# Output weights and two raw blocks loaded between the first two groups' values, with the first decode steps tied to the first group's chain

## The chip, the core and the metric

The kernel runs on one core of a Trainium2 chip. The metric is the device time of one execution, in microseconds (us). The core has TensorE (PE, matmuls), VectorE (DVE), ScalarE (ACT), GpSimd (POOL) and SyncE (SP), which here issues nearly all DMA transfers. Each engine works through its own list of instructions in order, and an instruction that waits for a semaphore holds up everything behind it on that engine.

## What is computed

Three layers follow one another for a batch of B = 8 sequences of S = 576 tokens (cut from the reference):

```python
# 1. packed attention: 8 heads of 64, 32 packed queries p per head
p_packed = softmax(p @ k.T / 8) @ v
x = softmax(q @ p_packed.T / 8) @ p_packed           # (8, 576, 512)
# 2. four experts of causal attention, head size 64; the top 2 of 4 by gate
for e in range(4):
    a = causal_softmax((x @ wq[e]) @ (x @ wk[e]).T / 8)
    out += gate[e] * (a @ (x @ wv[e]) @ wo[e])
# 3. a channel mix with token shift
xk = mu_k * x + (1 - mu_k) * x_prev;  xr = mu_r * x + (1 - mu_r) * x_prev
result = sigmoid(xr @ w_r) * (relu(xk @ w_k) ** 2 @ w_v)
```

`w_k`, `w_v` and `w_r` arrive as 64-bit floats, so the kernel reads them as pairs of 32-bit words ("raw" blocks) and decodes them.

## The kernel before

The first half (to about 410 us) runs the attention and the experts, batch by batch. A batch has two groups of four heads. The function `front` carries one group through a chain of small steps that pass from engine to engine: scores against the packed queries (`s1`, PE), their maximum and exponential (DVE, ACT), transposes `aT` (PE, ACT), the values (`vn`, PE) to `pp` (DVE), its transpose `ppT` (PE, ACT), the second scores `s2` of the queries `qT` (PE), their 32x32 transposes to the tile `st` (DVE, L303), maximum, subtraction (L308), exponential (ACT), sums, scaling, a transpose to `a2` and a split of it into two parts `A2h` (ACT) and `A2l` (DVE, L329). `PWh` and `PWl` (L315) come from the weights `wa` in the same way. After both groups, `values` (L352) and `project` (L407) use these on PE; `project` hands the queries and keys to `soft` (L466) by copies on ACT, DVE and POOL (`qs`, in `evac`, L202) and four small DMAs (L428, L429).

Beside this, `fold` multiplies the output weights `wo` into `w_k` and `w_r`. It loads `wo` into the tile `won`, splits it on POOL into `woTh` (L202) and `woTl` (L646), and then takes the weight in blocks of 128 rows and 256 columns. For a block, `decode` (L598) reads a `raw` tile: four DVE steps `dce`, `dcx`, `dce`, `dcu` (L611 to L620), an addition on POOL (`dcx`, L626), a square on ACT (`dcq`, L630), and a last DVE step that writes the block into `wc` (L640). Then POOL splits `wc` into `wh` and `wl`, and PE multiplies (L695). The tiles `won` and `wc` share one buffer (tag `wc`, one copy), so the first write to `wc` waits until POOL has finished with `won`. After four blocks of a piece POOL splits scaled blocks once more (`wh` x4 and `wl` x4) for a second set of matmuls.

The second half multiplies by `w_r` (L854), `w_k` (L874) and `w_v` (L915).

The order in which steps are written comes from a list sorted by times in units of an expert's block: `add(kind, generator, times)`; `FOLD_T` and `FOLD_N` give the fold's times, 13 of them up to 10.15. The tile framework then schedules the instructions of each engine by priorities and an estimate of its own, so a step need not stand where its time says. The first batch's front steps have a high priority (`PR0`), its loads are all written at the first step, and the DMAs run through eight completion semaphores in turn: a ninth DMA is issued only when the first has landed.

Of the kernel before, what the change touches and what calls it, by code (L numbers as in the profile page):

```python
# [9 lines left out]
F32 = mybir.dt.float32  # L10
# [3 lines left out]
AF = mybir.ActivationFunctionType  # L14
ALU = mybir.AluOpType
# [15 lines left out]
OUT_LAG = [3.85, 4.64, 7.81]  # L31
FOLD_T = [-20.0, 10.15, 107.63]
FOLD_N = 13
WA_AT = -28.3
# [17 lines left out]
def f32(ap):  # L52
    return ap.bitcast(F32)
# [3 lines left out]
def kernel(  # L57
# [4 lines left out]
    nc = tc.nc  # L62
    P = 128
# [9 lines left out]
    NDT = DM // P  # L73
# [21 lines left out]
    def nm(s):  # L95
        uid[0] += 1
        return f"{s}_{uid[0]}"
# [43 lines left out]
    if True:  # L141
# [59 lines left out]
        def pool_copy(o, x):  # L201
            nc.gpsimd.tensor_scalar(o, x, 1.0, 0.0, op0=ALU.mult, op1=ALU.add)  # L202

        def evac(eng, o, x):
            if eng == "A":
                nc.scalar.copy(o, x)  # L206
            elif eng == "V":
                nc.vector.tensor_copy(o, x)
            else:
                pool_copy(o, x)  # L210

# [18 lines left out]
        def load(b, gs):  # L230

            for g in gs:
                pT = pTs[(b * NG + g) % 2]
                nc.sync.dma_start(pT, p[b, g].rearrange("d j n -> d (j n)"))
                kT = ld.tile([P, NH, SH], F32, tag="kT", name=nm("kT"))
                nc.sync.dma_start(kT, k[b, g])
                loaded[b, g] = [pT, kT]
            for g in gs:
                vn = vns[(b * NG + g) % 2]
                nc.sync.dma_start(  # L240
                    vn[:, : NT - 1, :], v[b, g, : (NT - 1) * P].rearrange("(c p) x -> p c x", p=P)
                )
                nc.sync.dma_start(vn[TAIL:, NT - 1, :], v[b, g, (NT - 1) * P :])
                qT = ld.tile([P, NH, SH], F32, tag="qT", name=nm("qT"))
                nc.sync.dma_start(qT, q[b, g])
                loaded[b, g] += [vn, qT]

        def front(b, g):
# [33 lines left out]
            for c in range(NT):  # L282
# [7 lines left out]
            pp = fr.tile([P, 2, D], F32, tag="pp", name=nm("pp"))  # L290
            nc.vector.tensor_scalar(
                pp, ps[:, :D].unsqueeze(1).to_broadcast([P, 2, D]), ri, None, op0=ALU.mult
            )
            yield
            ps = one()
            nc.tensor.transpose(ps[:, :P], pp.rearrange("p x d -> p (x d)"), ident)
            ppT = fr.tile([P, P], F32, tag="ppT", name=nm("ppT"))
            evac(E_PPT, ppT, ps[:, :P])
# [8 lines left out]
            small = nc.gpsimd if b else nc.vector  # L307
            small.tensor_tensor(  # L308
                st3, st3, m2.unsqueeze(2).to_broadcast([P, NCB, NPK]), op=ALU.subtract
            )  # L310
            nc.scalar.activation(st, st, AF.Exp, scale=SC)
            yield
# [13 lines left out]
            a2 = fr.tile([P, S], F32, tag="sa", name=nm("a2"), bufs=4)  # L326
            nc.vector.transpose(a2, st)
            evac("P" if b else "A", bat["A2h"][:, g, :], a2)
# [269 lines left out]
        def decode(dst, src, r0, f0, raw=None):  # L598

            if src.dtype != I64:
# [7 lines left out]
            }  # L610
            nc.vector.tensor_scalar(  # L611
                t["e"], hi, 3, 0x3FFFFFF8, op0=ALU.logical_shift_left, op1=ALU.bitwise_and
            )
            nc.vector.scalar_tensor_tensor(
# [14 lines left out]
            if E_SQ == "A":  # L629
                nc.scalar.activation(f32(t["q"]), f32(hi), AF.Square)  # L630
            else:
                nc.gpsimd.tensor_mul(f32(t["q"]), f32(hi), f32(hi))
# [22 lines left out]
        def fold():  # L655

            won = dv.tile([P, NDT, 2 * P], F32, tag="wc", name=nm("won"), bufs=1)
            nc.sync.dma_start(won, wo.rearrange("(c p) n -> p c n", p=P))  # L660
            woT = {x: dv.tile([P, NDT, 2 * P], F32R, name="woT" + x, bufs=1) for x in "hl"}
# [5 lines left out]
            for n_, src, f0, m in PIECES:  # L667
                wc, wh, wl = quad()
                for c in range(NDT):
                    decode(wc[:, c, :], src, c * P, f0)  # L670
                    split(wh[:, c, :], wl[:, c, :], wc[:, c, :])
                    yield
# [66 lines left out]

        bats, loaded = {}, {}  # L740
        steps = []
# [196 lines left out]
        swap = max(last, FOLD_T[2] + 0.1)  # L938
        add("k", call(swap_w), [swap])
# [150 lines left out]
```

## Time and profile before

| | us |
|---|---|
| median of 3 runs | 827.92 |
| lowest and highest of these | 823.35, 831.87 |
| the profiled execution: its time | 830.5 |
| the profiled execution: its span | 828.7 |

The rows further on come from that one profiled execution. Its time is 1.8 us more than its span, which the profile does not show. Each engine's busy time, the chain of waits and a timeline of instructions by start time are views of the same trace. Line numbers are those of the kernel before.

### The profile page before, as it was taken

Reading aid. Unit: us, or ns where it says so; the run is one execution under the profiler, and the core shown is the slowest. Engines: PE = TensorE matmul, PEld = TensorE weight load, DVE = VectorE, ACT = ScalarE, POOL = GpSimd, SP = SyncE. Lnnn points to the kernel's source line nnn. Section 1 sums busy time; section 2 is a strip of 40 time slices with the busy share of each in tenths; the row PEclk is TensorE's granted clock in tenths of the full one; section 3 lists DMA queues with packets and bytes.
Section 4 is the critical chain, followed back from the end, with each engine's and each line's share of the span. In section 5 each row is a group of like instructions: output and inputs, shape, how many; then the busy total and the mean of one; then the engine's idle time right before and its main releaser. Section 6 shows DMA issues by size and latency. Waiting matters only on the chain.

```text
span 828.7 us, 15307 instructions
## 1 busy us (share of the span) xinstructions
PE 774.5 (93%) x5504; PEld 623.5 (75%) x5504; DVE 485.7 (59%) x1172; ACT 479.6 (58%) x1093; POOL 380.8 (46%) x490
## 2 busy tenths in 40 slices
PE   5388999999999899989899899999999999999998
PEld 4176877859678596868677778888888888888886
DVE  1979787786868767675764777787584111111111
ACT  2258768677686777787743523242678855565400
POOL 4647757484674735233601236171166343434510
PEclk8579999999999999999999989999999999999999
DMA  9646383564745345112744958586889755555521
GB/s 323 208 137 204 115 229 113 159 182 119 202 123 168 106 126 168 49 49 78 222 146 140 335 205 292 181 275 202 310 281 309 231 170 183 190 152 185 150 66 51
DMA packets 89835, 147.81 MB, mean 178 GB/s; under 512 B 6816, under 2 KB 61600, under 8 KB 87456
## 3 DMA queue, kind: packets, MB, share of 16 engines
q1 hardware_dynamic: 89616, 146.84, 56.1%
q8 instruction: 44, 0.72, 0.4%
q14 instruction: 31, 0.25, 0.1%
q10 hardware_dynamic: 144, 0.00, 0.0%
HBM read 87.04 MB, written 50.33 MB: 166 GB/s over the span
## 4 chain that ended last, share of the span: by engine, by line
PE 68%; DVE 13%; DMA 8%; ACT 6%; issue 2%; POOL 2%; SPq 1%; DVEq 0%; POOLq 0%; ACTq 0%
PE one L915 24%; PE big L874 8%; PE one L874 8%; PE one L548 4%; PE big L407 4%; PE one L854 3%; PE one L352 3%; PE one L695 3%; DVE ms L478 3%; DMA dl<-dscr 3%; ACT ms L482 2%; PE one L466 2%; PE big L854 2%; PE one L505 2%; DMA won<-in_wo_dram 1%
## 5 line engine op out<-in xcount | busy, mean ns | idle before, releaser
L920 DVE TENSOR_TENSOR ring<-one,ring 128x512 f32<-128x512 f32 x36 | 24.9, 692 | 168.8 <-PE one L915 161.4
L915 PE MATMUL one<-wvh,yh 128*128 128x512 f32 x288 | 112.0, 389 | 0.0
L915 PE MATMUL one<-wvl,yh 128*128 128x512 f32 x288 | 112.0, 389 | 0.0
L915 PE MATMUL one<-wvh,yl 128*128 128x512 f32 x288 | 112.0, 389 | 0.0
L482 ACT ACTIVATE ms<-ms,nb 64x64 f32<-64x64 f32 (+4 forms) x160 | 89.5, 560 | 26.1 <-DVE nb L478 24.1
L206 ACT COPY tb<-one 64x128 f32<-64x128 f32 (+5 forms) x208 | 64.0, 354 | 20.3 <-PE one L512 19.4
L548 PE MATMUL one<-tb,vg 128*64 128x320 f32 (+4 forms) x448 | 64.9, 379 | 6.5 <-ACT tb L206 4.3
L626 POOL TENSOR_TENSOR dcx<-dcx,dcu 128x256 f32<-128x256 f32 x40 | 30.6, 765 | 83.7 <-DVE dcu L620 72.0
L213 POOL TENSOR_TENSOR yl<-yvh,yh 128x1024 fp32r<-128x1024 f32 (+1 forms) x24 | 49.1, 2064 | 43.3 <-ACT yh L900 25.5
L478 DVE CUSTOM_DVE_ANT_0 ms<-one,mstrip 64x64 f32<-64x64 f32 (+3 forms) x128 | 51.7, 421 | 18.6 <-PE one L466 16.4
L915 PEld LDWEIGHTS one<-wvh,yl 128*128 128x128 f32 x288 | 54.1, 188 | 11.3
L915 PEld LDWEIGHTS one<-wvl,yh 128*128 128x128 f32 x288 | 54.1, 188 | 11.3
L915 PEld LDWEIGHTS one<-wvh,yh 128*128 128x128 f32 x288 | 54.1, 188 | 11.0
L548 PEld LDWEIGHTS one<-tb,vg 128*64 128x64 f32 x448 | 37.0, 140 | 31.6 <-ACT tb L206 6.9
L505 PE MATMUL one<-ident,ms 128*128 128x128 f32 x320 | 56.0, 284 | 3.9 <-ACT tb L206 2.6
L213 POOL TENSOR_TENSOR yl<-yvl,yh 128x1024 fp32r<-128x1024 f32 x16 | 38.2, 2399 | 41.2 <-ACT yh L900 19.7
L505 PEld LDWEIGHTS one<-ident,ms 128*128 128x128 f32 x320 | 38.2, 142 | 20.8 <-ACT tb L206 7.0
L213 POOL TENSOR_TENSOR dt<-cb 128x192 f32<-128x192 f32 (+1 forms) x48 | 29.9, 652 | 34.8 <-DVE cb L565 18.4
L466 PE MATMUL one<-ks,qs 128*128 128x64 f32 (+3 forms) x128 | 41.7, 350 | 2.3 <-ACT aT L206 0.9
L630 ACT ACTIVATE dcq<-raw 128x256 f32<-128x256 f32 x40 | 17.5, 437 | 42.1 <-DMA raw<-in_w_v_dram 19.2
L466 PE MATMUL one<-kl,qs 128*128 128x64 f32 (+3 forms) x128 | 40.3, 315 | 0.0
L1037 ACT ACTIVATE ring<-ring 128x1024 f32<-128x1024 f32 x18 | 19.1, 1061 | 35.4 <-DMA ring<-rscr 35.4
(206 smaller groups left out, 2084.2 us busy)
## 6 DMA issues: line engine op xcount, KB each, us to landing
yscr<-y SPq DMA_DIRECT2D x48, 384.0 KB, 3.5
dl<-dscr SPq DMA_DIRECT2D x40, 256.0 KB, 5.4
yvh<-yscr SPq DMA_DIRECT2D x10, 1024.0 KB, 5.7
kT<-in_k_dram SPq DMA_DIRECT2D x16, 576.0 KB, 4.5
qT<-in_q_dram SPq DMA_DIRECT2D x16, 576.0 KB, 5.1
rscr<-rr SPq DMA_DIRECT2D x12, 768.0 KB, 4.6
ring<-rscr SPq DMA_DIRECT2D x36, 256.0 KB, 2.9
out_dram<-ring SPq DMA_DIRECT2D x36, 256.0 KB, 3.2
```

Source lines behind the costliest of these rows:

```text
L206: nc.scalar.copy(o, x)
L213: nc.gpsimd.tensor_tensor(o, x, y, op=op)
L407: nc.tensor.matmul(ps[:, 512 * hf : 512 * hf + SH], ww[:, g, :], xx[:, g, :], start=i == 0, stop=i == 3 * NG - 1,)
L466: nc.tensor.matmul(ps[:, po : po + kn], qs[:, i * P : i * P + P], keys[:, ko : ko + kn], start=x == 0, stop=x == 1,)
L478: nc.vector.tensor_tensor_reduce(halves(mv) if last else mv, sv, halves(mk) if last else mk, op0=ALU.add, op1=ALU.min, scale=-SC, scalar=3 ...
L482: nc.scalar.activation(mv, mv, AF.Exp, bias=nb[p0:], scale=-1.0, accum_out=bat["sums"][p0:, i, e : e + 1],)
L505: nc.tensor.transpose(ps[:, at + j * P : at + (j + 1) * P], ms[:, j * P : (j + 1) * P], ident)
L548: nc.tensor.matmul(av[64 * ee : 64 * ee + 64, qo - lo : hi - lo], vg[:, j, HD * (2 * ep + ee) : HD * (2 * ep + ee + 1)], tslice(tabs[ee], ...
L626: nc.gpsimd.tensor_add(f32(t["x"]), f32(t["x"]), f32(t["u"]))
L854: nc.tensor.matmul(po, dx[:, NS * t + s, t0 : t0 + P], wpart("r", s, wx, t), start=n == 0, stop=n == 3 * KT - 1,)
L874: nc.tensor.matmul(po.rearrange("p (b n) -> p b n", b=2), wpart("k0" if f < 4 else "k1", s, wx, t)[:, f % 4 * P : f % 4 * P + P], dx[:, :, ...
L915: nc.tensor.matmul(ps, a[:, f, P * t : P * t + P], wres["v"][b][:, f, :], start=n == 0, stop=n == 3 * NFT - 1,)
```

## The change

The DMAs of `won` and of the first two raw blocks are issued inside `load`, ahead of the second group's values and queries in the first batch. `mark` remembers five instructions of the first group's chain: on DVE the `pp` step, the subtraction in `st` and the transpose to `a2`, on ACT the copy to `ppT` and the exponential in `st`. The first DVE step and the ACT step of the first four decodes are placed behind one of them on their engine (`tc.issue_after`): on DVE block 0 behind `pp`, block 1 behind the subtraction, blocks 2 and 3 behind the transpose; on ACT blocks 0 and 1 behind `ppT`, blocks 2 and 3 behind the exponential. The first 13 fold times are listed one by one.

```diff
-FOLD_T = [-20.0, 10.15, 107.63]
-FOLD_N = 13
+FOLD_0 = [-24.0, -20.0, -19.0, -14.9, -12.5, -8.3, -6.0, -4.0, -2.5, -0.5, 1.5, 3.5, 6.5]
+FOLD_T = [10.15, 107.63]
...
             for g in gs:
+                if b == 0 and g == 1:
+                    first["won"] = dv.tile([P, NDT, 2 * P], F32, tag="wc", name=nm("won"), bufs=1)
+                    nc.sync.dma_start(first["won"], wo.rearrange("(c p) n -> p c n", p=P))
+                    first["raw"] = [fetch_raw(w_k, c * P, 0) for c in range(2)]
                 vn = vns[(b * NG + g) % 2]
...
+        def mark(b, g, eng, x, ins):
+
+            if b == 0 and g == 0:
+                for turn in {"V": [(0,), (1,), (2, 3)], "A": [(0, 1), (2, 3)]}[eng][x]:
+                    first[eng, turn] = ins.ins
...
+        def behind(ins):
+            return tc.issue_after(ins) if ins is not None else nullcontext()
+
+        def decode(dst, src, r0, f0, raw=None, turn=None):
...
-            nc.vector.tensor_scalar(
-                t["e"], hi, 3, 0x3FFFFFF8, op0=ALU.logical_shift_left, op1=ALU.bitwise_and
-            )
+            with behind(first["V", turn] if turn is not None else None):
+                nc.vector.tensor_scalar(
+                    t["e"], hi, 3, 0x3FFFFFF8, op0=ALU.logical_shift_left, op1=ALU.bitwise_and
+                )
...
-                nc.scalar.activation(f32(t["q"]), f32(hi), AF.Square)
+                with behind(first["A", turn] if turn is not None else None):
+                    nc.scalar.activation(f32(t["q"]), f32(hi), AF.Square)
...
-                    decode(wc[:, c, :], src, c * P, f0)
+                    decode(wc[:, c, :], src, c * P, f0, first["raw"].pop(0) if first["raw"] else None, c if f0 == 0 and m == 0 else None)
...
-        add("fold", fold(), even(FOLD_T[0], FOLD_T[1], FOLD_N) + even(FOLD_T[1], FOLD_T[2], NFOLD - FOLD_N))
+        add("fold", fold(), FOLD_0 + even(FOLD_T[0], FOLD_T[1], NFOLD - len(FOLD_0)))
```

On SyncE's list, from the first group's values on (`vn`, `qT`: values and queries; `wa`: the input weights), before:

```order
L240 DMA vn_125<-in_v_dram 128x4x256
L243 DMA vn_125<-in_v_dram 64x256
L245 DMA qT_166<-in_q_dram 128x1152
L240 DMA vn_126<-in_v_dram 128x4x256
L243 DMA vn_126<-in_v_dram 64x256
L245 DMA qT_170<-in_q_dram 128x1152
L196 DMA wa<-in_w_in_dram 128x1544 x2
L660 DMA won_220<-in_wo_dram 128x4x256
L761 DMA raw_313<-in_w_k_dram 128x512
L761 DMA raw_372<-in_w_k_dram 128x512
L234 DMA pT_127<-in_p_dram 128x128
```

and changed:

```order
L243 DMA vn_125<-in_v_dram 128x4x256
L246 DMA vn_125<-in_v_dram 64x256
L248 DMA qT_166<-in_q_dram 128x1152
L240 DMA won_168<-in_wo_dram 128x4x256
L774 DMA raw_170<-in_w_k_dram 128x512
L774 DMA raw_172<-in_w_k_dram 128x512
L243 DMA vn_126<-in_v_dram 128x4x256
L246 DMA vn_126<-in_v_dram 64x256
L248 DMA qT_176<-in_q_dram 128x1152
L196 DMA wa<-in_w_in_dram 128x1544 x2
L233 DMA pT_127<-in_p_dram 128x128
```

`won` and the two raw blocks moved from behind `wa` to ahead of the second group's values.

On VectorE's list, from the first group's `pp` step on (`dce`, `dcx`, `dcu`, `wc`: the decode; `st`, `m`: the first group's second scores and their maximum), before:

```order
L291 TENSOR_SCALAR pp_253<-one_232,ri_15_191 128x128
L271 RECIPROCAL ri_23_218<-su_22_215 128x1
L611 TENSOR_SCALAR dce_316<-raw_313 128x256
L614 SCALAR_TENSOR_TENSOR dcx_315<-raw_313,dce_316 128x256
L617 TENSOR_SCALAR dce_316<-dcx_315 128x256
L620 SCALAR_TENSOR_TENSOR dcu_317<-raw_313,dce_316 128x256
L611 TENSOR_SCALAR dce_375<-raw_372 128x256
L303 STREAM_TRANSPOSE st_303<-big_294 128x288 x2
L291 TENSOR_SCALAR pp_284<-one_263,ri_23_218 128x128
L306 TENSOR_REDUCE m_37_306<-st_303 128x18
L640 SCALAR_TENSOR_TENSOR wc_310<-dcq_318,dcx_315 128x256
L308 TENSOR_TENSOR st_303<-st_303,m_37_306 128x576
```

and changed:

```order
L300 TENSOR_SCALAR pp_265<-one_244,ri_18_197 128x128
L624 TENSOR_SCALAR dce_318<-raw_170 128x256
L280 RECIPROCAL ri_26_226<-su_25_223 128x1
L627 SCALAR_TENSOR_TENSOR dcx_317<-raw_170,dce_318 128x256
L630 TENSOR_SCALAR dce_318<-dcx_317 128x256
L633 SCALAR_TENSOR_TENSOR dcu_319<-raw_170,dce_318 128x256
L654 SCALAR_TENSOR_TENSOR wc_314<-dcq_320,dcx_317 128x256
L312 STREAM_TRANSPOSE st_307<-big_298 128x288 x2
L300 TENSOR_SCALAR pp_292<-one_271,ri_26_226 128x128
L315 TENSOR_REDUCE m_39_310<-st_307 128x18
L317 TENSOR_TENSOR st_307<-st_307,m_39_310 128x576
L624 TENSOR_SCALAR dce_358<-raw_172 128x256
```

Block 0's whole decode, with its last step that writes `wc`, now stands ahead of the transposes to `st`; block 1's first step, which stood ahead of them, now follows the subtraction.

On GpSimd's list, where `project` hands over the first queries (`qs`; `wh`, `wl`: the second split of the first piece), before:

```order
L626 TENSOR_TENSOR dcx_916<-dcx_916,dcu_918 128x256
L202 TENSOR_SCALAR qs_112<-qs_112 64x576
L202 TENSOR_SCALAR wh_311<-wc_310 128x256 x4
L646 TENSOR_TENSOR wl_312<-wc_310,wh_311 128x256 x4
L626 TENSOR_TENSOR dcx_965<-dcx_965,dcu_967 128x256
L202 TENSOR_SCALAR qs_113<-qs_113 64x576
```

and changed:

```order
L639 TENSOR_TENSOR dcx_869<-dcx_869,dcu_871 128x256
L202 TENSOR_SCALAR wh_315<-wc_314 128x256 x4
L660 TENSOR_TENSOR wl_316<-wc_314,wh_315 128x256 x4
L202 TENSOR_SCALAR qs_112<-qs_112 64x576
L639 TENSOR_TENSOR dcx_965<-dcx_965,dcu_967 128x256
L202 TENSOR_SCALAR qs_113<-qs_113 64x576
```

The eight splits of the first piece moved from behind the copy of `qs` to ahead of it.

## Rows read from the trace of the kernel before

**Rows 1.** The page's first part: busy time of each engine, its share of the span, instructions.

```profile
PE 774.5 (93%) x5504; PEld 623.5 (75%) x5504; DVE 485.7 (59%) x1172; ACT 479.6 (58%) x1093; POOL 380.8 (46%) x490
```

**Rows 2.** Busy time by stage of the span, four stretches (busy us and instructions of each engine).

```profile
0.00:60.00 60.00, 35.80 (x388) 25.84 (x389) 35.19 (x85) 18.91 (x39) 31.04 (x67) 0.72 0.69 224
60.00:400.00 340.00, 321.21 (x3242) 254.87 (x3241) 258.55 (x792) 255.48 (x749) 190.91 (x307) 0.98 0.49 140
400.00:500.00 100.00, 92.50 (x446) 73.96 (x445) 67.57 (x109) 46.15 (x104) 26.21 (x28) 0.95 0.59 207
500.00:828.00 328.00, 324.95 (x1434) 268.83 (x1432) 124.42 (x188) 159.05 (x203) 132.68 (x88) 1.00 0.62 201
```

**Rows 3.** The chain of waits, 0 to 75 us: start, length, what.

```profile
9.38 11.88 DMA won<-in_wo_dram
...
21.34 1.72 POOL woTh L202 x4
23.06 3.00 POOL woTl L646 x4
26.06 0.69 POOL dcx L626
...
26.78 0.43 DVE wc L640
...
50.64 2.76 PE big L407 x21
```

**Rows 4.** The timeline, 0 to 44 us: start, length, instruction, idle before it.

```profile
15.04 0.65 PE L284 MATMUL one<-vn,aT 128*32 128x64 f32 x30 [0.73 <-ACT aT L206]
...
15.61 1.21 PE L222 MATMUL big<-qT,ppT 64*32 64x288 f32 x16
...
21.96 0.30 DVE L611 TENSOR_SCALAR dce<-raw 128x256 int32<-128x256 int32 x1 [8.07 <-DMA raw<-in_w_k_dram]
...
24.72 0.83 DVE L303 STREAM_TRANSPOSE st<-big 128x288 f32<-128x288 f32 x2
...
35.21 0.95 DVE L315 TENSOR_TENSOR PWl<-big,PWh 128x772 fp32r<-128x772 f32 x1
```

**Rows 5.** DMA issues of 4.3-5.5, 7.4-8.2 and 9.3-9.7 us: size, us to landing.

```profile
vn<-in_v_dram SPq DMA_DIRECT2D x1, 512.0 KB, 8.5
...
wa<-in_w_in_dram SPq DMA_DIRECT2D x1, 772.0 KB, 12.2
...
won<-in_wo_dram SPq DMA_DIRECT2D x1, 512.0 KB, 11.9
```

**Rows 6.** The timeline of SyncE's queue, 0 to 45 us.

```profile
4.33 1.18 SPq L240 DMA_DIRECT2D vn<-in_v_dram  x1
...
9.38 0.38 SPq L660 DMA_DIRECT2D won<-in_wo_dram  x1
```

**Rows 7.** VectorE's groups of instructions, 20 to 46 us: busy us, mean ns, idle before.

```profile
L611 DVE TENSOR_SCALAR dce<-raw 128x256 int32<-128x256 int32 x5 | 2.5, 496 | 8.1 <-DMA raw<-in_w_k_dram 8.1
...
L640 DVE SCALAR_TENSOR_TENSOR wc<-dcq,dcx 128x256 f32<-128x256 f32 x4 | 1.6, 412 | 0.3 <-POOL dcx L626 0.3
```

**Rows 8.** The timeline, 44 to 62 us.

```profile
44.55 1.09 DVE L329 TENSOR_TENSOR A2l<-a,A2h 128x576 fp32r<-128x576 f32 x1
...
53.02 0.68 POOL L202 TENSOR_SCALAR qs<-qs 64x576 fp32r<-64x576 f32 x1 [4.13 <-ACT qs L419]
...
54.27 1.52 POOL L202 TENSOR_SCALAR wh<-wc 128x256 fp32r<-128x256 f32 x4 [0.58 <-PE one L695]
...
55.75 2.81 POOL L646 TENSOR_TENSOR wl<-wc,wh 128x256 fp32r<-128x256 f32 x4
...
58.83 0.27 PE L466 MATMUL one<-ks,qs 128*128 128x64 f32 x1 [0.95 <-ACT aT L206]
```

**Rows 9.** Granted clock by stretches of 2 us (the PEclk column, share of full speed).

```profile
16.00:18.00 2.00, 1.39 (x26) 0.39 (x10) 0.00 (x0) 0.00 (x0) 0.00 (x0) 0.50 1.02 371
...
50.00:52.00 2.00, 2.00 (x18) 2.00 (x17) 0.32 (x2) 1.14 (x5) 0.00 (x0) 1.00 0.83 293
```

More of the change, by code (lines that the diff above doesn't have):

```diff
@@ L1 @@
 import math
-from contextlib import ExitStack
+from contextlib import ExitStack, nullcontext
 import concourse.bass as bass
@@ L205, in evac @@
             if eng == "A":
[L206 to L210, printed above, removed]
+                return nc.scalar.copy(o, x)
+            if eng == "V":
+                return nc.vector.tensor_copy(o, x)
+            pool_copy(o, x)
         def pool_tt(o, x, y, op):
@@ L290, in front @@
             pp = fr.tile([P, 2, D], F32, tag="pp", name=nm("pp"))
-            nc.vector.tensor_scalar(
+            mark(b, g, "V", 0, nc.vector.tensor_scalar(
                 pp, ps[:, :D].unsqueeze(1).to_broadcast([P, 2, D]), ri, None, op0=ALU.mult
-            )
+            ))
             yield
@@ L297, in front @@
             ppT = fr.tile([P, P], F32, tag="ppT", name=nm("ppT"))
-            evac(E_PPT, ppT, ps[:, :P])
+            mark(b, g, "A", 0, evac(E_PPT, ppT, ps[:, :P]))
             yield
@@ L307, in front @@
             small = nc.gpsimd if b else nc.vector
-            small.tensor_tensor(
+            mark(b, g, "V", 1, small.tensor_tensor(
                 st3, st3, m2.unsqueeze(2).to_broadcast([P, NCB, NPK]), op=ALU.subtract
-            )
-            nc.scalar.activation(st, st, AF.Exp, scale=SC)
+            ))
+            mark(b, g, "A", 1, nc.scalar.activation(st, st, AF.Exp, scale=SC))
             yield
@@ L326, in front @@
             a2 = fr.tile([P, S], F32, tag="sa", name=nm("a2"), bufs=4)
-            nc.vector.transpose(a2, st)
+            mark(b, g, "V", 2, nc.vector.transpose(a2, st))
             evac("P" if b else "A", bat["A2h"][:, g, :], a2)
@@ L596, in fetch_raw @@
             return raw
-        def decode(dst, src, r0, f0, raw=None):
+        def behind(ins):
+            return tc.issue_after(ins) if ins is not None else nullcontext()
+        def decode(dst, src, r0, f0, raw=None, turn=None):
             if src.dtype != I64:
@@ L610, in decode @@
             }
-            nc.vector.tensor_scalar(
-                t["e"], hi, 3, 0x3FFFFFF8, op0=ALU.logical_shift_left, op1=ALU.bitwise_and
-            )
+            with behind(first["V", turn] if turn is not None else None):
+                nc.vector.tensor_scalar(
+                    t["e"], hi, 3, 0x3FFFFFF8, op0=ALU.logical_shift_left, op1=ALU.bitwise_and
+                )
             nc.vector.scalar_tensor_tensor(
@@ L655, in fold @@
         def fold():
-            won = dv.tile([P, NDT, 2 * P], F32, tag="wc", name=nm("won"), bufs=1)
-            nc.sync.dma_start(won, wo.rearrange("(c p) n -> p c n", p=P))
+            won = first["won"]
             woT = {x: dv.tile([P, NDT, 2 * P], F32R, name="woT" + x, bufs=1) for x in "hl"}
@@ L736, in call @@
             yield
-        bats, loaded = {}, {}
+        bats, loaded, first = {}, {}, {}
         steps = []
@@ L936 @@
         add("front", zeros(), [-6.0 + 0.5 * i for i in range(7)])
-        add("fold", fold(), even(FOLD_T[0], FOLD_T[1], FOLD_N) + even(FOLD_T[1], FOLD_T[2], NFOLD - FOLD_N))
-        swap = max(last, FOLD_T[2] + 0.1)
+        add("fold", fold(), FOLD_0 + even(FOLD_T[0], FOLD_T[1], NFOLD - len(FOLD_0)))
+        swap = max(last, FOLD_T[1] + 0.1)
         add("k", call(swap_w), [swap])
```

## The prediction

> **What bounds the kernel now.** The page first: TensorE is busy for 774.5 us of the span, 93% [rows 1], so most of the run can only be shortened by taking its idle time away. The table by stage says where that idle time is. In the first 60 us TensorE works 35.80 us, so it idles 24.2; in the next 340 us it idles 18.8, in the 100 after that 7.5, and in the last 328 only 3.1 [rows 2]. From 60 us on there is little slack anywhere, so a microsecond won or lost in the first 60 should be found again at the end, unless the later order changes.
>
> Then the chain of waits in that stage. It is not made of TensorE's work: it goes through the landing of the output weights (11.88 us, from 9.38 on), eight splits on GpSimd (1.72 and 3.00), its addition for block 0 (0.69), and the write of `wc` on VectorE (0.43) [rows 3]. The timeline shows the queue behind that. The second scores of the first group have been on TensorE from 15.61 for 1.21 us, ready at 16.8. Their transposes to `st` on VectorE start only at 24.72, because block 0's decode stands ahead of them and its first step waited 8.07 us for the raw block, to 21.96 [rows 4]. So VectorE, with finished scores at hand, sits behind a transfer that belongs to the fold. From the transposes on it works nearly without a pause to the end of the second group's `A2l` at 45.64 [rows 8]; the batch's dense matmuls follow, and the first scores of the experts start at 58.83 [rows 8].
>
> **The change part by part.** All times are on the profiled execution: span 828.7, time 830.5.
>
> *The transfers.* The output weights take the eighth place in the queue, which the second group's values have now. Those are 512 KB too, issued at 4.33 [rows 6] and landed 8.5 us later [rows 5], at 12.8. So `won` lands at about 12.8 in place of 21.3. The last part of `wa` lands now 12.2 us after an issue near 7.6 [rows 5], at 19.8; between the two, 64 KB of values, 576 of queries and 1,544 of `wa` came in 7.0 us, about 310 KB per us. At that rate the two raw blocks (512 KB) are there 1.6 us after `won`, at 14.4. In exchange 1 MB, or 3.3 us, stands ahead of the second values, their queries and `wa`, whose last part lands at about 23. VectorE first needs it for `PWl`, now at 35.21, 10.5 us behind the transposes [rows 4]. With transposes at 18.8 (below) that is 29.3, so some 6 us are left for the matmuls and the copy between: the delay of `wa` is hidden by the VectorE steps that stand before; without them each microsecond of it would count.
>
> *Block 0 and the transposes to `st`.* The tie puts the decode behind `pp`, but not behind the transposes, and its last step, the write of `wc`, has moved from behind them to ahead of them. This write waits for GpSimd to finish with `won`, since the two share a buffer. That is a new wait; behind it on VectorE stands all of the first group's chain. Its time: landing 12.8, splits 1.72 + 3.00, addition 0.69, write 0.43, which gives 18.6, with hand-overs 18.8. The other condition is the scores: the second values, whose matmuls stand ahead of the scores on TensorE, land 3.3 us later, at 16.1, and 0.65 for them and 1.21 for the scores [rows 4] follow, 18.0. So the wait for `won` ends last, at 18.8, and the transposes come 24.72 - 18.8 = 5.9 us earlier.
>
> *From there to `A2l`.* VectorE does the same steps of the chain in both orders. Of the decode, the first step of block 1 (0.50 mean) now lies behind the transposes, while the write of block 0 (0.41 mean) and the first step of the fifth block (0.50) [rows 7] no longer lie between: 0.4 us less. `A2l` should end at 45.64 - 5.9 - 0.4 = 39.3, which is 6.3 earlier. The ties of blocks 2 and 3 only order work that VectorE does anyway; I price them at nothing, since VectorE is full there and the raw transfers for them have several microseconds of lead. Should one be late, it costs what it lacks.
>
> *From `A2l` to the first scores.* Here something is given back. GpSimd now does the second splits of the first piece (1.52 + 2.81 us) ahead of the copy of `qs`, which before came first, at 53.02 [rows 8]. The splits wait for the first fold matmuls to end, 54.27 before, which is 8.6 us after `A2l`. In the new order 21 matmuls of `project` (2.76 [rows 3]) come behind these fold matmuls and not ahead: 8.6 - 2.8 = 5.8, so they end at 45.1, the splits at 49.4, the copy at 50.1. Before it ended at 53.70: this link gains only 3.6 us. TensorE has other work meanwhile (the second pair's projection now stands before the first scores), so not all of the difference is lost. Bounds 3.6 and 6.3; I take 5.0, the middle.
>
> *The rest of the run.* Some 260 of 4,562 TensorE entries change places, small swaps within the fold's time and again around the weight change after 400 us. No row prices that. With 18.8 us of idle time between 60 and 400 [rows 2], I take nothing, with 3 us either way for the range.
>
> The sum: 830.5 - 5.0 = 825.5, or 0.6% less. On the median of 827.92 that is 823.0.
>
> The Trainium skill has a rule against this change, in "Perfetto Trace Analysis", section "Identifying the Most-Contended Engine": improve the engine with the highest occupancy first. That is TensorE, and the change takes no work off it; by the rule alone the time would stay at 827.9. The trace agrees with the rule from 60 us on and not before, where TensorE idles for 24 us.
>
> **The rivals.** *Nothing is left at the end: 827.9.* The experts' first scores come earlier, but VectorE and ScalarE then take the work at their own pace, or the swaps later cost as much. For it: from 60 to 400 us these two are busy 259 and 255 us of 340, and the chain there runs through all engines. Against it: a pipeline limited by any of its engines still ends earlier when it is fed earlier.
>
> *The clock also gains: 819.5.* TensorE's granted clock is at 0.50 from about 16 us (1.2 GHz) and back at 1.00 (2.4 GHz) by 50 [rows 9], while the dense matmuls begin when `A2l` ends. From 45.64 to 50 they run at half speed, 4.4 us, of which 2.2 would be saved at full speed. TensorE's gap behind the first scores shrinks from about 8 us to 2, so the clock might be up sooner. With the upper bound of the chain, 6.3 + 2.2 = 8.5. Against it: the clock fell while the chain ran as densely as it will, and the gaps further on stay.
>
> *The new wait decides, and it is slower: 830.4.* If `won` does not land in the order of issue, the write of `wc` holds the transposes. They come no earlier than now if the landing is at 24.72 - 5.95 = 18.8 or later; with the landing at 21.3 as before, they start at 27.2 and the run is 2.5 us longer. Against it: the transfers of this trace landed in the order in which they were issued, at 12.8, 19.8 and 21.3 [rows 5, 6]. The Trainium skill, "DMA: Bandwidth & Descriptors", section "Queues, rings and completion order", says that completion is not in order for one issuing engine. By that the late landing would be open; this trace shows no case of it among these transfers.
>
> *The tie does not do what it says.* In part this is so already: block 0 stands whole ahead of the transposes. It is in the sum, with 0.8 us lost against scores that are ready at 18.0, so it makes no case of its own.
>
> **How the numbers follow.** The forecast, 821.6 to 824.3 from the two bounds, has 0.55; no gain 0.20; with the clock 0.15; slower 0.10. Three runs before spread from 823.35 to 831.87, so a few microseconds of the measurement and 3 us for the later swaps come on top; the range is 816.5 to 829.5, which leaves out half of the clock's case and most of the slower one. About 1% is what a measurement can tell from no change here: below 819.6 is faster, above 836.2 slower. Nearly all the forecast, the case without gain and the slower rival, whose price is only 0.3%, lie within 1%. Faster gets the clock's case and a small part of the forecast: 0.18. Slower, which needs more than any rival gives, gets 0.04; the rest, 0.78, is the same.
>
> **What would show it.** In the profile after: `won` landed near 13, and GpSimd's first split there; VectorE's `st` transposes at about 18.8, directly behind the write of `wc`; `A2l` of the second group ending near 39; the copy of `qs` behind eight splits at about 50; the first scores near 54; TensorE's idle time in the first 60 us some 5 us less. The prediction is wrong if `won` lands late, if the third or fourth raw block or `wa` shows up as a wait on the chain, or if the 5 us are there at 60 us and gone at 400.

## The result, and the profile after

The changed kernel takes 819.51 us by the median of 5 runs (816.46 to 820.48), the kernel before 826.03 beside it: a ratio of 0.9895, with a 95% interval of 0.9857 to 0.9932. In a second set of 6 runs (below) it was 817.22 against 827.89, 0.9865 (0.9833 to 0.9897). So it is faster by 1.0 to 1.4%, inside the predicted range, by 6.5 to 10.7 us by the medians where the forecast said 5.

The profiled execution has a span of 818.7 us, 10.0 less than before. From its page, the busy times (TensorE's work is what it was [rows 1]):

```profile
PE 773.4 (94%) x5504; PEld 622.1 (76%) x5504; DVE 483.2 (59%) x1172; ACT 477.7 (58%) x1093; POOL 380.2 (46%) x490
```

The table by stage that answers to [rows 2] (busy us and instructions of PE, PEld, DVE, ACT, POOL; then the granted clock):

```profile
0.00:60.00 60.00, 42.66 (x444) 31.59 (x448) 38.49 (x106) 21.87 (x50) 32.77 (x70) 0.72 0.70 235
60.00:400.00 340.00, 319.99 (x3223) 254.04 (x3213) 255.83 (x782) 253.63 (x748) 191.18 (x310) 0.98 0.49 142
400.00:500.00 100.00, 95.79 (x467) 76.01 (x465) 68.66 (x107) 47.33 (x102) 27.70 (x28) 1.00 0.64 228
500.00:818.00 318.00, 314.91 (x1390) 260.44 (x1388) 120.19 (x180) 154.87 (x196) 128.57 (x85) 1.00 0.61 197
```

TensorE idles 17.3 us of the first 60 in place of 24.2, and 4.2 of the stage from 400 to 500 in place of 7.5, where its clock is now 1.00 and was 0.95. So there are two gains, and the second is one that the prediction had not priced.

The timeline of the start, which answers to [rows 4]:

```profile
13.30 1.73 POOL L202 TENSOR_SCALAR woTh<-won 128x256 fp32r<-128x256 f32 x4 [3.46 <-DMA won<-in_wo_dram]
13.94 0.29 DVE L624 TENSOR_SCALAR dce<-raw 128x256 int32<-128x256 int32 x1 [0.51 <-DMA raw<-in_w_k_dram]
...
17.03 1.07 PE L293 MATMUL one<-vn,aT 128*32 128x64 f32 x30 [2.45 <-DMA vn<-in_v_dram]
18.03 1.21 PE L221 MATMUL big<-qT,ppT 64*32 64x288 f32 x16
18.70 0.43 DVE L654 SCALAR_TENSOR_TENSOR wc<-dcq,dcx 128x256 f32<-128x256 f32 x1 [2.66 <-POOL dcx L639]
...
19.35 0.85 DVE L312 STREAM_TRANSPOSE st<-big 128x288 f32<-128x288 f32 x2 [0.23 <-PE big L221]
...
28.91 0.43 ACT L644 ACTIVATE dcq<-raw 128x256 f32<-128x256 f32 x1 [6.30 <-DMA raw<-in_w_k_dram]
...
30.06 0.96 DVE L324 TENSOR_TENSOR PWl<-big,PWh 128x772 fp32r<-128x772 f32 x1 [2.66 <-ACT PWh L323]
```

The output weights are there at 13.3, the transposes start at 19.35 (24.72 before). New is the wait ahead of `PWl`: ScalarE sits 6.30 us on the third raw block, and `PWh` stands behind that. The load of this block is issued only at 20.87. SyncE's waits up to 30 us say what held it (us in total, times, longest):

```profile
SPq L774 <- DMA wa<-in_w_in_dram: 1.2, 1, 1.2
```

The eighth DMA ahead of it, the first part of `wa`, landed at 20.79 and gave its semaphore back; the raw block's buffer had been read to the end at 16.04. Further on, the rows that answer to [rows 8]:

```profile
39.52 0.75 DVE L338 TENSOR_TENSOR A2l<-a,A2h 128x576 fp32r<-128x576 f32 x1
...
47.09 1.51 POOL L202 TENSOR_SCALAR wh<-wc 128x256 fp32r<-128x256 f32 x4 [2.90 <-PE one L708]
48.57 2.83 POOL L660 TENSOR_TENSOR wl<-wc,wh 128x256 fp32r<-128x256 f32 x4
...
51.48 0.98 POOL L202 TENSOR_SCALAR qs<-qs 64x576 fp32r<-64x576 f32 x1
...
55.37 0.19 PE L475 MATMUL one<-ks,qs 128*128 128x64 f32 x1
```

`A2l` ends 5.4 us earlier (40.27 for 45.64), the copy of `qs` only 1.2 (52.46 for 53.70), the first scores 3.5. In the second traces of the two kernels (below) it is 3.9 (40.36 for 44.21), 1.0 (50.86 for 51.82) and 3.7 us.

Now the weight change, where `w_k` (`wk0l`, `wk1l`: loaded by SyncE, then cast by ScalarE to `wk0h`, `wk1h`) takes the place of the attention's buffers, while TensorE works on `w_r` (`rstage`) in blocks that are loaded into `dl` and cast to `dh`. Timeline of the kernel before, with the last store of `dt` to `dscr` first:

```profile
455.78 0.38 SPq L582 DMA_DIRECT2D dscr<-dt  x1
457.07 0.52 SPq L761 DMA_DIRECT2D dl<-dscr  x1
458.48 0.33 SPq L864 DMA_DIRECT2D rscr<-rr  x1
458.85 3.19 SPq L761 DMA_DIRECT2D wk0l<-wscrk  x4
...
465.86 1.05 ACT L768 CAST wk0h<-wk0l 128x1024 fp32r<-128x1024 f32 x1 [2.72 <-DMA wk0l<-wscrk]
...
467.12 3.37 SPq L761 DMA_DIRECT2D dl<-dscr  x3
...
475.29 0.73 PE L854 MATMUL big<-wrh,dh 128*128 128x512 f32 x2 [2.16 <-DVE rr L839]
475.81 1.05 ACT L768 CAST wk1h<-wk1l 128x1024 fp32r<-128x1024 f32 x1
...
477.59 2.12 ACT L823 CAST dh<-dl 128x512 fp32r<-128x512 f32 x3 [0.73 <-DMA dl<-dscr]
478.26 1.22 PE L854 MATMUL one<-wrh,dh 128*128 128x512 f32 x2 [0.99 <-ACT dh L823]
479.28 1.05 PE L854 MATMUL one<-wrl,dh 128*128 128x512 f32 x2
```

and of the changed kernel:

```profile
447.07 0.38 SPq L591 DMA_DIRECT2D dscr<-dt  x1
447.50 2.15 SPq L774 DMA_DIRECT2D wk0l<-wscrk  x4
...
452.60 2.26 ACT L781 CAST wk0h<-wk0l 128x1024 fp32r<-128x1024 f32 x2 [1.19 <-DMA wk0l<-wscrk]
...
464.81 1.05 ACT L781 CAST wk1h<-wk1l 128x1024 fp32r<-128x1024 f32 x1
...
465.79 2.79 ACT L836 CAST dh<-dl 128x512 fp32r<-128x512 f32 x4
466.46 0.73 PE L867 MATMUL one<-wrh,dh 128*128 128x512 f32 x2 [0.71 <-ACT dh L836]
467.03 0.62 PE L867 MATMUL one<-wrl,dh 128*128 128x512 f32 x2
```

Before, the loads of `w_k` stand behind a block load and a store of gates; three more block loads (`dl` x3) stand behind them in turn, and their casts behind the eight `w_k` casts. TensorE waits 2.16 and 0.99 us, and then its pairs of matmuls take 1.05 us in place of 0.62. After, the loads of `w_k` follow the last store directly and TensorE waits 0.71 us in all. The table by stretches of 6 us (the granted clock is the third number from the end), before:

```profile
470.00:476.00 6.00, 3.84 (x17) 2.88 (x16) 5.13 (x6) 4.81 (x6) 3.66 (x2) 1.00 1.02 405
476.00:482.00 6.00, 5.01 (x14) 3.43 (x13) 3.76 (x2) 3.03 (x5) 6.00 (x3) 0.54 1.07 393
```

and after:

```profile
464.00:470.00 6.00, 5.29 (x24) 4.05 (x23) 5.19 (x6) 3.94 (x6) 5.73 (x3) 1.00 1.06 402
```

That is 2.4 us of waits (3.15 against 0.71) and a stretch at 1.2 GHz: from 476.3 to 483.4 seven pairs of matmuls take 0.89 to 1.22 us each in place of 0.62, and most stand 0.85 us apart in place of 0.45, which costs about 2.8 us.

### The profile page after: what moved, and what is told of

Read it like the earlier page. It is cut to its first block, busy times and chain, and to the rows that moved or that the text cites. A ratio compares the mean times of both kernels' runs of the same rounds, so it can differ in the third digit from the quotient of the medians.

```text
span 818.7 us, 15299 instructions
## 1 busy us (share of the span) xinstructions
PE 773.4 (94%) x5504; PEld 622.1 (76%) x5504; DVE 483.2 (59%) x1172; ACT 477.7 (58%) x1093; POOL 380.2 (46%) x490
## 4 chain that ended last, share of the span: by engine, by line
PE 75%; DVE 10%; ACT 6%; DMA 5%; issue 2%; POOL 1%; SPq 0%; DVEq 0%; ACTq 0%; POOLq 0%
PE one L928 24%; PE big L887 8%; PE one L887 8%; PE one L557 6%; PE big L416 5%; PE big L867 3%; PE one L867 3%; PE one L475 3%; PE one L708 3%; PE one L361 3%; PE one L514 3%; DVE ms L487 2%; ACT ms L491 2%; PE big L221 2%; DMA raw<-in_w_k_dram 2%
## 5 line engine op out<-in xcount | busy, mean ns | idle before, releaser
L212 POOL TENSOR_TENSOR dt<-cb 128x192 f32<-128x192 f32 (+1 forms) x48 | 29.6, 645 | 35.8 <-DVE cb L574 17.3
```

What stands on the lines that cost most here:

```text
L212: nc.gpsimd.tensor_tensor(o, x, y, op=op)
```

## The experiments

The theory at this point: about 5 us come from the early loads at the start, and as much from the order at the weight change, which moves as a by-product. The rivals: all of it comes from the start, and the loss at the weight change was one execution's chance; or the ties, not the loads, carry the start.

Executions of the kernel before lie between 823.35 and 833.44 us, so two landmarks of each trace separate the two places; between two traces of one kernel they differ by up to 3.3 us, and the other kernels have one trace each. Three of the traced executions lie at an edge of their runs: the changed kernel's first (820.48) and late_order_in_before's (822.57) are the slowest, that of loads_without_ties (814.35) is the fastest. "11th store" is the start of the eleventh of the sixteen stores of `dt`, in the sixth batch; "rest" is the time from there to the first matmul with `w_v`, behind the weight change. Times in us; the ratios compare with runs of the kernel before on the same chip, whose medians were 828.2, 828.9 and 827.9 in the three sets.

| kernel | median | ratio (95%) | `st` transposes | first scores | 11th store | rest |
|---|---|---|---|---|---|---|
| before | 826.03 | | 24.72 | 58.83 | 336.23 | 292.72 |
| before_again | 828.81 | one run | 23.31 | 57.47 | 333.55 | 293.72 |
| changed | 819.51 | 0.9895 (0.9857 to 0.9932) | 19.35 | 55.37 | 331.51 | 287.40 |
| after_again | 817.22 | 0.9865 (0.9833 to 0.9897) | 19.11 | 53.77 | 328.22 | 287.66 |
| times_alone | 823.43 | 0.9941 (0.992 to 0.9962) | 24.46 | 59.48 | 333.31 | 289.16 |
| ties_without_loads | 821.99 | 0.9919 (0.9891 to 0.9947) | 23.95 | 57.38 | 332.08 | 289.07 |
| loads_without_ties | 817.83 | 0.9878 (0.9851 to 0.9905) | 23.38 | 54.39 | 326.83 | 285.97 |
| late_order_in_before | 820.88 | 0.9914 (0.9894 to 0.9935) | 23.89 | 58.70 | 335.43 | 285.59 |
| wk_first_in_before | 825.73 | 0.9976 (0.9953 to 0.9998) | 24.51 | 57.58 | 334.31 | 290.21 |
| late_order_undone | 817.06 | 0.9872 (0.9848 to 0.9897) | 19.25 | 52.92 | 328.78 | 286.44 |
| qs_on_vector | 820.05 | 0.9901 (0.9876 to 0.9926) | 18.34 | 54.20 | 330.23 | 288.24 |
| raw2_behind_pwh | 817.54 | 0.9872 (0.9844 to 0.9901) | 19.33 | 52.47 | 328.29 | 287.96 |
| raw2_and_late_order | 814.27 | 0.9828 (0.98 to 0.9857) | 18.46 | 51.83 | 327.21 | 285.79 |
| loads_and_late_order | 816.11 | 0.984 (0.9805 to 0.9875) | 22.35 | 54.96 | 330.80 | 284.72 |

**The two kernels again.** No edit, a second trace of each.

> The kernel before, unchanged, for a second trace. If the loss at the weight change belongs to its order, TensorE's waits of 2 to 3 us near 475 us and the drop of the granted clock behind them show again; if it was one execution's chance, they don't. The other drops of the clock (near 177, 282, 375 and 406 us in the first trace) should move from execution to execution.

> The changed kernel, unchanged, for a second trace and five more runs beside the other three. By the theory now (about 4.7 us from the start and 5 to 5.5 from the weight change) it is 9 to 10 us faster than the kernel before, 0.988 to 0.9895, with TensorE waiting about 0.7 us at the weight change and no drop of its clock there. If the first measurement of 0.9895 was a low draw of the kernel before, 0.992 or more.

The loss at the weight change is there again in the kernel before:

```profile
473.62 0.93 PE L854 MATMUL big<-wrh,dh 128*128 128x512 f32 x2 [3.00 <-DVE rr L839]
474.35 1.06 PE L854 MATMUL big<-wrl,dh 128*128 128x512 f32 x2
...
477.20 1.22 PE L854 MATMUL one<-wrh,dh 128*128 128x512 f32 x2 [0.94 <-ACT dh L823]
```

It waits 3.94 us and runs at half clock from 474; the changed kernel waits 1.02 us in its second trace and keeps its clock. So the loss belongs to the order, clock included: it is in both traces of the one kernel and in neither of the other. after_again's 0.9865 is a little better than expected. Two traces against two: the 11th store is 5.0 us earlier (329.87 against 334.89), the rest 5.7 us shorter (287.5 against 293.2). Together 10.7, which is the difference of the mean spans too (827.85 and 817.2). The difference in the rest lies where the weights change: it starts behind the fifteenth store (418.74 to 422.12 us before, 414.31 to 417.47 changed), from which the first matmul with `w_v` is 206.8 and 208.5 us away before, 201.4 and 201.6 changed; and it ends ahead of the first matmul with `w_k`, from which it is 130.6 us in every trace.

**Only the new fold times.** Loads as before, no ties:

```diff
-                    first["won"] = dv.tile([P, NDT, 2 * P], F32, tag="wc", name=nm("won"), bufs=1)
-                    nc.sync.dma_start(first["won"], wo.rearrange("(c p) n -> p c n", p=P))
-                    first["raw"] = [fetch_raw(w_k, c * P, 0) for c in range(2)]
...
-            won = first["won"]
+            won = dv.tile([P, NDT, 2 * P], F32, tag="wc", name=nm("won"), bufs=1)
+            nc.sync.dma_start(won, wo.rearrange("(c p) n -> p c n", p=P))
...
-                    decode(wc[:, c, :], src, c * P, f0, first["raw"].pop(0) if first["raw"] else None, c if f0 == 0 and m == 0 else None)
+                    decode(wc[:, c, :], src, c * P, f0, None, None)
```

> Only the new fold times: the output weights and raw blocks are loaded where the kernel before loads them and nothing is tied. SyncE's list at the start is that of the kernel before but for four places, and the list at the weight change is that of the changed kernel. Theory (about half of the gain is the order at the weight change and has nothing to do with the start): the transposes to st stay at 24.7 us, the batches are within 1 us of the kernel before until 420 us, and then 4 to 6 us are won between 440 and 490 us: 820.5 to 822.5 by the median. Rival (all of the gain comes from the start, and what the weight change shows is one execution's chance): 826, no gain at 490 us either.

The transposes stay at 24.46, the first scores at 59.48 are no earlier than before, the 11th store is where before_again has it; the rest is 3.6 to 4.6 us shorter. So thirteen times of the fold's first steps give about half of the gain, 0.9941, and give it beyond 400 us; 823.43 us is a little more than the 820.5 to 822.5 expected. The rest is 1.6 us longer than the changed kernel's 287.5. In this trace the clock is at half from 404 to 411 us, and TensorE waits 1.52 us near 470; what share each has in the 1.6 us isn't shown.

**Ties and times without the loads.** As above, but the last argument of `decode` stays.

> The changed kernel's ties and fold times, with the output weights and raw blocks loaded where the kernel before loads them. Theory (the loads make the start, the ties nothing): VectorE still waits for the first raw block to about 22 us, the transposes to st start at 24 us or later, the batches are within 1.5 us of the kernel before until 420 us, and the weight change gives its 5 us: 0.993 to 0.995. Rival (the ties carry the start's gain): 0.988 to 0.9895, as the changed kernel.

VectorE still waits at the same place, 8.07 us in [rows 4]:

```profile
21.93 0.29 DVE L620 TENSOR_SCALAR dce<-raw 128x256 int32<-128x256 int32 x1 [8.31 <-DMA raw<-in_w_k_dram]
```

0.9919, a little better than expected: the rest gives 4.1 us, the 11th store 1.5 to 4.2 us against the two traces before. By the time alone the rival is not quite out, since the interval begins at 0.9891. By the start it is: the transposes (23.95) lie between the two traces before, and the first scores (57.38) are 0.1 us before the earlier of them.

**Loads without the ties.**

```diff
-                    decode(wc[:, c, :], src, c * P, f0, first["raw"].pop(0) if first["raw"] else None, c if f0 == 0 and m == 0 else None)
+                    decode(wc[:, c, :], src, c * P, f0, first["raw"].pop(0) if first["raw"] else None, None)
```

> The changed kernel without its ties: the early transfers and the new fold times stay, the order at the weight change is that of the changed kernel. VectorE's list now has block 0 and two steps of block 1 ahead of the first group's pp and block 1's write of wc ahead of the transposes to st. Theory (the transfers give the start, the ties keep the decode out of VectorE's way, the order at the weight change gives the rest): the transposes start near 22 us, between the 24.72 of the kernel before and the 19.35 of the changed one; the batches from the fifth on are 1.5 to 3 us ahead of the kernel before in place of 4.7; with the 5 us at the weight change 819 to 821 by the median, 1 to 3 us above the changed kernel. Rival (the transfers alone do it, the ties are idle): transposes at 19.4 and the time of the changed kernel.

Neither: the transposes start at 23.38, later than the theory had them, and yet the time is that of the changed kernel: 0.9878 lies between its two measurements. The timeline shows how:

```profile
23.38 0.85 DVE L312 STREAM_TRANSPOSE st<-big 128x288 f32<-128x288 f32 x2 [0.58 <-PE big L221]
...
39.53 1.05 PE L708 MATMUL one<-wl,woTh 128*128 128x256 f32 x4
...
42.39 2.01 POOL L202 TENSOR_SCALAR wh<-wc 128x256 fp32r<-128x256 f32 x4
...
43.36 0.78 DVE L338 TENSOR_TENSOR A2l<-a,A2h 128x576 fp32r<-128x576 f32 x1 [0.49 <-ACT A2h L206]
...
48.88 0.67 POOL L202 TENSOR_SCALAR qs<-qs 64x576 fp32r<-64x576 f32 x1 [1.67 <-ACT qs L428]
...
54.39 0.27 PE L475 MATMUL one<-ks,qs 128*128 128x64 f32 x1 [2.00 <-DMA ks<-ks]
```

With the decode in front, the fold's first matmuls run from 37 to 42.5, while TensorE would wait for `A2l`, and GpSimd's eight splits start at 42.39, not at 47.09. `A2l` ends 3.9 us later than in the changed kernel (44.14), but from there to the first scores it takes 10.3 us instead of 15.1 (13.4 in after_again). The reading is that the early loads bring the fold's first piece in good time, and that it comes to the same whether this is spent on earlier transposes or on earlier fold matmuls.

**The order at the weight change, put into the kernel before.**

```diff
-add("soft", call(soft, b, e, group), [t])
+add("soft", call(soft, b, e, group), [t], 300 if b == B - 1 else None)
-add("turn", call(turn, b, e, group), [t + TURN_LAG[i]])
+add("turn", call(turn, b, e, group), [t + TURN_LAG[i]], 300 if b == B - 1 else None)
-add("out", pair_out(b, ep), [t0 + 2 * NT * (ep + 1) + t for t in OUT_LAG])
+add("out", pair_out(b, ep), [t0 + 2 * NT * (ep + 1) + t for t in OUT_LAG], 400 if b == B - 1 else None)
```

> The kernel before, with a higher scheduling priority for the last batch's experts and last output pairs alone; the start is that of the kernel before. TensorE's last pair of outputs now stands ahead of the third pair of w_r stages, and the w_k loads stand directly behind the last dscr store, as in the changed kernel. Theory: nothing until 440 us, then 4 to 6 us won between 440 and 490 us with TensorE's clock at full there: 820 to 822. Rival (chance, or the gain needs the earlier start): within 1 us of the kernel before.

0.9914, 7.1 us, all of it behind the 11th store (336.23 and 333.55 before, 335.43 here), with 0.69 us of waits at the weight change and the clock up. The gain doesn't need the earlier start.

**The order undone in the changed kernel.**

```diff
-add("out", pair_out(b, ep), [t0 + 2 * NT * (ep + 1) + t for t in OUT_LAG])
+add("out", pair_out(b, ep), [t0 + 2 * NT * (ep + 1) + t for t in OUT_LAG], -50 if b == B - 1 and ep else None)
```

> The changed kernel with a lower scheduling priority for the last output pair of the last batch: its last two matmuls stand behind nine of the following w_r stages, and the w_k loads behind two stores of gates and four block loads, much as in the kernel before. The start is that of the changed kernel. Theory: the 4.7 us up to 420 us stay, and most of the further 5 us go: 822 to 825 by the median, 3 to 6 us above the changed kernel. Rival (the gain at the weight change is not made by this order): the changed kernel's time within 1 us.

The theory missed: 817.06, no loss at all. The loads of `w_k` are late here, but a whole `w_r` block is loaded and cast ahead of them:

```profile
450.05 1.65 SPq L774 DMA_DIRECT2D dl<-dscr  x2
...
453.27 3.25 SPq L774 DMA_DIRECT2D wk0l<-wscrk  x4
454.48 1.33 ACT L836 CAST dh<-dl 128x512 fp32r<-128x512 f32 x2 [0.94 <-DMA dl<-dscr]
...
459.48 1.05 ACT L781 CAST wk0h<-wk0l 128x1024 fp32r<-128x1024 f32 x1 [0.65 <-DMA wk0l<-wscrk]
```

TensorE waits 0.71 us. So late loads of `w_k` alone make no loss, and neither does a late last pair of outputs. A whole `w_r` block is cast here before the `w_k` casts begin, where in the kernel before three of a block's four loads stand behind the `w_k` loads; in the changed kernel the `w_k` loads and casts come early. The next block's casts stand behind the `w_k` casts in this kernel too, from 471.38 on, and cost the 0.71 us. That the loss comes from a block split by late `w_k` loads is a reading, which the next run tries.

**Only the loads of `w_k` forward, in the kernel before.**

```diff
-add("gates", call(rstage, i, t0), [(swap + R_RUN[i] if early else end + i + 1.5) + 0.05 * x])
+add("gates", call(rstage, i, t0), [(swap + R_RUN[i] if early else end + i + 1.5) + 0.05 * x], -50 if i == 2 else None)
```

> The kernel before, with the third w_r block's stages at a lower scheduling priority. The start is that of the kernel before, and TensorE's last pair of outputs still stands behind ten of the w_r matmul pairs; but on SyncE's list the eight w_k loads now stand directly behind the last dscr store, two rows of gates and block loads earlier, and on ScalarE the casts of the next block are no longer all behind the eight w_k casts. Theory as it stands after the first four runs (the 3.15 us of waits and the lower clock at 470 to 490 us come from a w_r block that is loaded and cast behind the late w_k loads, wherever the output pair stands): TensorE's waits there fall from 3.15 to about 0.7 us, and if the clock stays up too, the run is 2.4 to 5.5 us faster than before: 823 to 826. Rival (the place of the last output pair on TensorE decides): within 1 us of the kernel before.

The clock stays up, and the waits are smaller but four: 0.65, 0.82, 0.39 and 0.60, 2.46 together. The rest is 2.5 to 3.5 us shorter, the run 0.9976, 2 us, at the low end or just under what was expected; the interval (0.9953 to 0.9998) doesn't shut out the rival's 1 us. By the waits and the clock, the order of the loads is part of the cause. What the other part is stays open: late_order_in_before has 7 us with the priorities of the last batch's experts and outputs raised together, and no run raises one of them alone. The place of the last pair of outputs doesn't explain it by itself, since late_order_undone has that pair late without a loss.

**The link from `A2l` to the first scores.** The first copy of `qs` on VectorE:

```diff
-evac(E_Z, z[64:, 1, :], f32(z[64:, 0, :]))
+evac(E_Z if b or ep else "V", z[64:, 1, :], f32(z[64:, 0, :]))
```

> The changed kernel with the first copy of qs on VectorE, behind the subtraction that reads qs, and so no longer behind the eight splits on GpSimd. If the prediction's link holds (A2l gains more than the first scores, since the splits stand ahead of the copy): the copy ends about 0.8 us behind that subtraction in place of 2.4, the first scores come 1.5 us earlier against the stage's other work, and the run is 1 to 1.5 us faster than the changed kernel: 0.988 of the kernel before. Rival (TensorE fills the gap with the second pair's projection, so the link costs nothing): the changed kernel's 0.9895 again.

The copy now ends 1.0 us behind the subtraction, and then the next condition shows, the keys' DMA:

```profile
48.42 0.96 DVE L208 CAST qs<-qs 64x576 fp32r<-64x576 f32 x1
...
54.20 0.27 PE L475 MATMUL one<-ks,qs 128*128 128x64 f32 x1 [2.08 <-DMA ks<-ks]
```

0.9901: nothing is won, as the rival has it. The splits ahead of the copy are a link, but not one that costs time.

**The third raw block.** The mark moves from the exponential to the copy behind it:

```diff
-            mark(b, g, "A", 1, nc.scalar.activation(st, st, AF.Exp, scale=SC))
+            nc.scalar.activation(st, st, AF.Exp, scale=SC)
...
-            nc.scalar.copy(halves(bat["PWh"][:, g, :]), ps)
+            mark(b, g, "A", 1, nc.scalar.copy(halves(bat["PWh"][:, g, :]), ps))
```

> The changed kernel, with ScalarE's step of the third and fourth block tied behind the copy to PWh in place of the exponential, so that the wait for the third raw block (6.30 us on ScalarE) no longer stands ahead of PWh. Theory (that wait is a cost of the change which the prediction put at nothing, and the eight splits limit what it is worth): PWl starts 2 us earlier, A2l 1.5 to 2.5 us earlier, the first scores at most 1 us earlier: 0.988 to 0.9895 of the kernel before. Rival (the chain through A2l sets the end): 2.5 us faster than the changed kernel, 0.9865. Second rival (the wait is hidden): A2l where it was.

The wait no longer stands ahead of `PWh`, and `A2l` starts 1.9 us earlier (39.52 and 39.62 in the changed kernel):

```profile
27.32 0.95 DVE L324 TENSOR_TENSOR PWl<-big,PWh 128x772 fp32r<-128x772 f32 x1
28.82 0.44 ACT L644 ACTIVATE dcq<-raw 128x256 f32<-128x256 f32 x1 [4.13 <-DMA raw<-in_w_k_dram]
...
37.60 0.75 DVE L338 TENSOR_TENSOR A2l<-a,A2h 128x576 fp32r<-128x576 f32 x1
```

The first scores come at 52.47, 1.3 us before after_again, a little more than expected. The 11th store is where after_again has it (328.29 and 328.22), and 0.9872 lies between the two measurements of the changed kernel. What it is worth can't be told from nothing.

**Both together.** raw2_behind_pwh with the three priorities of late_order_in_before; and those priorities on loads_without_ties.

> Two edits on the changed kernel: ScalarE's step of the third and fourth block behind the copy to PWh, and the higher priority for the last batch's experts and outputs that won 7 us on the kernel before. If the two losses are separate and add up: 2 us at the start and 1 to 2 at the weight change below the changed kernel, 0.984 to 0.987, the fastest so far. If not: 0.987 to 0.9885.

> The changed kernel without any tie, with the same higher priority for the last batch. Theory (the ties bring the transposes 4 us forward but not the first scores, since the fold's second splits then stand ahead of the copy of qs): no slower than the kernel with ties and late order by more than 1 us, 0.985 to 0.9885. Rival (the ties are worth their 4 us): 4 us slower than that one, 0.989 to 0.992.

The first is the fastest of all, 814.27 us, 0.9828, and 3 us faster than the changed kernel beside it. The second, without ties, has 0.984 (0.9805 to 0.9875), within 2 us of it (1.8 by the medians, 1.0 by the ratios) where the theory had at most 1 and the rival 4. The shortest rests of the table are those of the three kernels with the priorities and of loads_without_ties, 284.7 to 286.0.

## Why the prediction was right, and what it mis-sized

*The transfers.* Right: `won` was forecast at 12.8 and is there at 13.3, the raw block 14.4 and 13.94 (issue and landing went in the same order again, so the slower rival had no case). *Block 0 and the transposes.* 18.8 forecast, 19.35 measured. The write of `wc` started at 18.70 and ended at 19.13, 0.3 us behind what was said. But not this wait ended last, as the prediction had it: the scores did, 0.2 us behind the write, since the second values landed near 17 and not at 16.1. *To `A2l`.* Forecast 6.3 us earlier, measured 5.4 and 3.9. That "the raw transfers for them have several microseconds of lead" was wrong for the third block: its load is issued at 20.87, when the first part of `wa` has landed, and `PWh` waits for it on ScalarE. The early loads had pushed `wa` back, which the prediction counted for `PWl` and not for the DMA eight places behind. By the prediction's own list (the third raw block as a wait on the chain) this is a sign of being wrong. It costs `A2l` 1.9 us and the run nothing that could be measured.

*From `A2l` to the first scores.* That only part of the gain passes was right. The 5.0 us were not found where they were forecast: in two traces against two the first scores are 3.6 us earlier, at the lower bound, the third store 0.3 and the seventh to the fourteenth 4.7 to 5.1. So the number is right from 235 us on, and in part by luck. Over all traces, the eight with early loads have the 11th store at 328.98 on average, the six without at 334.15: 5.2 us. And the way there was read too narrowly. The prediction took the gain from the transposes along the chain and let the eight splits limit it, with 3.6 us for the copy of `qs`; the copy gained 1.2 and 1.0. loads_without_ties has the same gain with transposes 4 us later, and qs_on_vector cuts the splits' link without any gain. The reading that fits both, not tested by itself: the fold's matmuls and the chain share TensorE and VectorE in this stage, and the sum of both, not one chain, sets the first scores.

*The later swaps.* This is the term that failed. "No row prices that ... I take nothing, with 3 us either way": it is 5.7 us, the larger half. The 7.5 us of idle time between 400 and 500 stood in [rows 2] beside a clock of 0.95; the waits near 475 us, 3.15 us with the half clock behind them, could have been read in the trace of before, and the order of the new kernel showed that the loads of `w_k` had moved just there. The prediction asked what the swaps would cost, and not what they would free.

*The clock rival, 819.5.* Its number came nearest, by the sum of two other things. At the start the clock comes back to full between 44 and 46 us in one trace of the changed kernel and between 40 and 42 in the other (48 to 50 and 46 to 48 before). From the end of `A2l` to there it is about 5 us in the first trace of the changed kernel and under 2 in the second (about 4 and 3 before), and the second trace's first scores are 1.6 us earlier. So something like the rival's gain shows in one execution and not in the other. Its larger effect was at the weight change, where no part of the prediction looked. The range doesn't leave out half of this case, as the prediction says: 819.5 lies 3 us inside.

The chances suffered with it: 0.18 for faster by over 1%, and the measurements say 1.0 and 1.4%, the second with its whole interval beyond 1%. The rule of the Trainium skill, "Perfetto Trace Analysis", section "Identifying the Most-Contended Engine", to optimize the engine with the highest occupancy first, was read as a rule against the change. It doesn't say that only less work for the engine would count, so the 827.9 was the prediction's own reading. Here that engine's work stayed (774.5 and 773.4 us busy) and 10 us of its idle and slow time went.

## What to carry to other kernels

Where a scheduler places instructions by priorities and its own estimates, a change at the start can move the end: compare the whole order, look in the trace of before at every stage where instructions changed places, and price the waits that stand there now. Split the gain by landmarks along the run and take two traces of each kernel, since one pair mixes places and executions. When a chain and a filler share the same engines, moving the chain's steps forward need not bring more than moving the filler out of the way: here, with and without the ties, the time was the same within 2 us. And where DMAs take turns on eight semaphores, as here, a load that is moved forward delays others, and with their landings the issue of the loads eight places behind them.

## What the runs showed of the hardware

Apart from the start and the last few us, the traces have one to five drops of the granted clock to half, each of a few us. Many follow a wait of 1.2 to 3.0 us on TensorE, some no wait that long. The same wait doesn't always bring one: the wait of 2.26 us for `tb` near 275 us was followed by a drop in the first trace of the kernel before and the first of the changed one, and in the second trace of neither. So two executions of one kernel differ: the first trace of the changed kernel has four such drops between 60 and 400 us and the second two, and its 11th store is 3.3 us later, 1.6 of them already at the first scores. Over all 14 traces a drop came with the 2.26 us wait for `tb` in six and with the wait of 2.0 us near 370 in eleven. In both traces of the kernel before one followed the waits near 474 us. Why a given wait does or doesn't is open.
